# A fused attention and two feed-forward layers: sums of v spread over steps, two last tiles kept whole, next batch's attention emitted earlier

## The chip, the cores and the metric

The kernel runs on one core of a Trainium2 chip. The metric is device time in microseconds, the median of several runs. One execution was also taken by the hardware profiler; its span and rows are what is read below. The kernel is written in a tile framework: the author emits instructions in program order, and a scheduler orders them on each engine by that order and by a simulated timeline, so that an instruction emitted later may run earlier where the simulation sees a gap.

## The reference

Inputs are q, k and v of 4 batches x 12 heads x 448 positions x 64, two gain vectors, and the weights of two layers.

```python
def rmsnorm(x, g):
    return x / np.sqrt(np.mean(x * x, axis=-1, keepdims=True) + 1e-06) * g
scores = matmul(rmsnorm(q, g_q), rmsnorm(k, g_k).transpose(0, 1, 3, 2)) / np.sqrt(64)
attn = exp(scores - max(scores)); attn = attn / (sum(attn) + 1e-09)
x = matmul(attn, v)                         # to 1792 tokens x 768
h = x @ moe_w_in                            # 768 x 2048
x = (h * sigmoid(1.702 * h)) @ moe_w_out    # 2048 x 768
h = x @ moe2_w_in
out = (max(h, 0) + alpha * min(h, 0)) @ moe2_w_out
```

The kernel computes each product from 16-bit halves: an operand is scaled and split into a high and a low part (`split`, one instruction on ScalarE and one on VectorE), and three matmuls stand for one. The scales need the largest absolute value of what is scaled, for v among others, batch by batch.

## The kernel before, in words

**Attention** goes by units. A pair P of heads has four units, and each unit is a tile of 128 queries (or 64) of both heads: scores on TensorE, maximum on VectorE, exponentials on ScalarE, and for batches 1 to 3 a split and a transpose by DMA (`pt`), then `values`. The generator `attention` does one unit per step, with later phases some steps behind. The first batch is done in two halves: `first_pairs` runs units 0 and 1 of its six pairs while the first layer's input weights are converted (`w1i_steps`); a second loop over `attention` runs units 2 and 3 while the output weights (`w1o_steps`) are converted and the first 256 columns of the first layer are formed (`first_in`). Both loops have 16 steps.

**Sums of v.** For batches 1 to 3 the scale of v comes from sums of absolute values. `v_scale(b)` takes a batch in 8 pieces: a load by the POOL queue into a two-buffer tile `vst` (L312), held behind the fifth group's norms, and an Abs with a running sum on ScalarE (L313). `later_v_scales` then reduces the columns, sends them through DRAM to all partitions (`v_line`, `vrow`) and forms `mv` and `av`. All this is emitted at step 8 of the second loop.

**First layer.** `first_moe1` forms the remaining columns of the first batch's 16 tiles m and splits each, then `moe1_out` does the output product (`yp`, L812), six tiles of 48 matmuls. Activations wait in place, two tiles further on in g; for the last two tiles there is no such place, and `raw_t` gives a `last_t` of 256 columns in the buffers of `vst`, copied (L768) into a whole tile before the rest is formed.

**Order around it.** The loop at the end takes one tick of the first layer (32 for the inner tiles, 24 for the output) and emits attention steps of the next batch so far that they are done at `PACE[b]` of the 56 ticks; for the first batch they start at tick `B1_AT` = 24. `moe1` of the next batch needs all its attention (x tiles, a pool of 9 slots, `NX`).

Of the kernel before, what the change touches and what calls it, by code (L numbers as in the profile page):

```python
# [24 lines left out]
VLAG = 0  # L25
LAG_ = 4
LAG2 = 5
PACE = (1.0, 1.0, 1.0, 1.0)
HOLD = 12800
M_AT = 2  # L30
VS_AT = 8
# [26 lines left out]
def attention_moe_kernel(  # L58
# [51 lines left out]
    def scaled_reciprocal(dst, src, c):  # L110

        nc.vector.tensor_scalar(out=dst, in0=src, scalar1=1.0 / c, scalar2=None, op0=ALU.mult)
        nc.vector.reciprocal(out=dst, in_=dst)
# [24 lines left out]
    def split(dst, src, scale):  # L138

        nc.scalar.activation(out=dst[0], in_=src, func=AF.Copy, scale=scale)  # L140
        nc.vector.scalar_tensor_tensor(  # L141
            out=dst[1], in0=src, scalar=scale, in1=dst[0], op0=ALU.mult, op1=ALU.subtract
        )
# [162 lines left out]
    def v_scale(b):  # L306
        flat = v[b].rearrange("h s d -> (h s d)").rearrange("(p n) -> p n", p=128)
        n = flat.shape[1] // VN
        col = vcols[:, b - 1]
        for i in range(VN):  # L310
            t = raw_p.tile([128, n], F32, tag="vst", name="vst")
            nc.gpsimd.dma_start(out=t, in_=flat[:, i * n:(i + 1) * n])  # L312
            nc.scalar.activation(out=t, in_=t, func=AF.Abs, accum_out=col[:, i:i + 1])  # L313

    def later_v_scales():
        n = B - 1
        one = small.tile([128, B - 1], F32, tag="vone", name="vmax")
        nc.vector.tensor_reduce(out=one, in_=vcols, op=ALU.max, axis=AX)
        pow2floor(one, one)
        line = dram.tile([128, n], F32, name="v_line")  # L320
        row = att_p.tile([128, 128 * n], F32, tag="sq", name="vrow", bufs=SQB)
        nc.sync.dma_start(out=line, in_=one)
        nc.sync.dma_start(out=row, in_=line.rearrange("p b -> (p b)").partition_broadcast(128))
        nc.vector.tensor_reduce(out=mv[:, 1:B], in_=row.rearrange("q (p b) -> q b p", b=n), op=ALU.max, axis=AX)
        scaled_reciprocal(av[:, 1:B], mv[:, 1:B], 2.0 ** 13)

    raws = {}
    rawv = {}
# [197 lines left out]
        probs[u] = (sp, nm, n)  # L526

    sums_of = {}
    spread = {}

    def exponent(u):
        sp, nm, n = probs[u]
        P, half, _, _ = unit(u)
        pr = [att_p.tile([128, S], F32, tag="p", name="pr", bufs=4) for _ in range(n)]
        if u < 4 * NP:
            if u % 2 == 0:
                sums_of[P, half] = small.tile([128, 4], F32, tag="sums", name="sums", bufs=3)
            sm = sums_of[P, half][:, 2 * (u % 2):2 * (u % 2) + n]
        else:
            sm = small.tile([128, 2], F32, tag="sm", name="sm", bufs=4)[:, 0:n]  # L540
        for i in range(n):
            nc.scalar.activation(  # L542
                out=pr[i], in_=sp[:, i, 0:S], func=AF.Exp, bias=nm[:, i:i + 1],
                scale=c_s if u >= 4 * NP else 1.0, accum_out=sm[:, i:i + 1]
            )
        if u >= 4 * NP:
            nc.scalar.activation(out=sm, in_=sm, func=AF.Copy, scale=2.0 ** -14, bias=1e-9 * 2.0 ** -14)
        elif u % 2:
            sm = sums_of[P, half][:, 0:2 + n]
            nc.vector.tensor_scalar(out=sm, in0=sm, scalar1=1e-9, scalar2=None, op0=ALU.add)  # L550
            nc.vector.reciprocal(out=sm, in_=sm)
        probs[u] = (pr, sm)
# [180 lines left out]
    def urgent(on):  # L733
        return tc.high_priority(on) if on else ExitStack()

    def first_in(cols, m, g, t):

        n = cols.stop - cols.start
        ps = ps_m.tile([128, n], F32, tag="m", name="hp")
        i = 0  # L740
        for kk in range(KD):
            for e, f in ((0, 0), (0, 1), (1, 0)):
                nc.tensor.matmul(  # L743
                    out=ps, lhsT=w1i[:, kk, e, m * 128:(m + 1) * 128], rhs=xs[0, kk][:, f, cols], start=(i == 0),
                    stop=(i == 3 * KD - 1)
                )
                i += 1
        dst = raw_t(g, m)[:, cols] if t is None else t[:, cols]
        if t is None:
            t = work.tile([128, S], F32, tag="t", name="t")  # L750
        with urgent(HP0):
            nc.scalar.activation(out=t[:, cols], in_=ps, func=AF.Tanh, scale=c_t[:, 0:1])
            nc.vector.scalar_tensor_tensor(out=dst, in0=t[:, cols], scalar=1.0, in1=ps, op0=ALU.add, op1=ALU.mult)  # L753
# [7 lines left out]
    def first_moe1(g):  # L761

        for m in range(KF):
            if m < KF - 2:
                first_in(slice(FIRST, S), m, g, None)
            else:
                t = work.tile([128, S], F32, tag="t", name="t")
                nc.vector.tensor_copy(out=t[:, 0:FIRST], in_=raw_t(g, m))  # L768
                first_in(slice(FIRST, S), m, g, t)
            if m == RAW0 - 1:  # L770
                for _ in w1o_steps:
                    pass
                split_g(g, range(RAW0))
            elif m >= RAW0:
                split_g(g, (m,), t if m >= KF - 2 else None)
            yield
            yield
        yield from moe1_out(0, g)
# [47 lines left out]
    def raw_t(g, m):  # L826

        if m < KF - 2:
            return g[:, m + 2].rearrange("p e t -> p (e t)").bitcast(F32)
        if m not in last_t:  # L830
            last_t[m] = raw_p.tile([128, FIRST], F32, tag="vst", name="last_t")
        return last_t[m]

    def split_g(g, ms, t=None):
        for m in ms:
            split((g[:, m, 0], g[:, m, 1]), raw_t(g, m) if t is None else t, scales["w1o"][1][:, m:m + 1])

    TICKS = 2 * KF + 4 * KD

# [330 lines left out]
    if True:  # L1170
# [36 lines left out]
            load_qk(P)  # L1207
        load_v(2)
        normalize(1)
        for _ in first_pairs():  # L1210
            for _ in range(W_RATE):
                next(w1i_steps, None)
        for _ in w1i_steps:
# [9 lines left out]
        for i, _ in enumerate(steps):  # L1223
            pairs = max(0, (i - LAG + 1) // 2)
            rows = KF - 2 if pairs >= 4 else (HOLD + pairs * HELD) // (2 * DM) - 2
            while n1o < min(1 + 2 * rows + 3 * (rows // 2), (i + 1) * W1O_RATE, 57):
                next(w1o_steps)
                n1o += 1
            if i >= M_AT and i - M_AT < KF:
                first_in(slice(0, FIRST), i - M_AT, g0, None)  # L1230
            if i == VS_AT:
                for b in range(1, B):
                    with tc.issue_after(rooted[4].ins):
                        v_scale(b)
                later_v_scales()
        while n1o < 57:
            next(w1o_steps)
            n1o += 1
        for m in range(len(range(2 * NP + LAG)) - M_AT, KF):
            first_in(slice(0, FIRST), m, g0, None)  # L1240
        with tc.issue_after(loads["w1o"][W1O_HOLD].ins):
            normalize(NP, NP + 1)
            for _ in prep_pair(NP):
# [52 lines left out]
```

## Time and profile before

| | us |
|---|---|
| median of 3 runs | 1156.42 |
| lowest, highest | 1152.11, 1162.04 |
| profiled execution, its own time | 1151.71 |
| span of the profile, first to last instruction | 1149.9 |

Busy in the span: TensorE 1058.2 us (92%), VectorE 804.3 (70%), ScalarE 680.6 (59%), GpSimd 176.7 (15%). A share of the whole span is an average over stages, so the rows below are taken by stretches. Rows of waits give the time that an engine stood idle and what ended that time.

### The profile page before, as it was taken

To read this page: it belongs to the slowest core of one execution; us is meant where nothing else is said; L and a number is where in the kernel's file an instruction comes from. 1 tells how busy PE (TensorE), PEld (TensorE's weight loads), DVE (VectorE), ACT (ScalarE), POOL (GpSimd) and SP (SyncE) were. 2 spreads that over 40 slices of the span, in tenths; PEclk is the share of its full clock that TensorE was granted. 3 is DMA by queue.
4 is the path that set the end of the run, shared out by engine and by line. 5 is a ranking of instruction groups with operands and counts; after the bars stand their busy time and mean duration, and the time that the engine had idled before them with its cause. 6 is when DMAs were issued, how large, how long until landed. Compare 5 with 4: busy or idle time off the path is not lost.

```text
span 1149.9 us, 18349 instructions
## 1 busy us (share of the span) xinstructions
PE 1058.2 (92%) x6752; PEld 579.9 (50%) x6752; DVE 804.3 (70%) x1392; ACT 680.6 (59%) x1396; POOL 176.7 (15%) x364
## 2 busy tenths in 40 slices
PE   3576898887979999999999999999999999999998
PEld 1343466643434554555555455444444477666664
DVE  6979899987868984577533956599977223968341
ACT  4688786877888876688632562356555324655220
POOL 2622003766424332200000000000000000000000
PEclk9677999999989999999999999999999999999999
DMA  7975553378886656644436701665442323363011
GB/s 228 273 196 144 168 150 105 97 145 186 187 173 137 149 126 153 126 109 110 88 112 210 243 1 64 222 216 188 158 156 83 137 70 113 101 186 104 32 32 28
DMA packets 235562, 158.25 MB, mean 138 GB/s; under 512 B 167888, under 2 KB 214736, under 8 KB 235472
## 3 DMA queue, kind: packets, MB, share of 16 engines
q1 hardware_dynamic: 229200, 141.41, 44.3%
q0 software_dynamic: 6272, 15.67, 5.6%
q8 instruction: 53, 0.87, 0.3%
q14 instruction: 37, 0.30, 0.1%
HBM read 92.41 MB, written 25.69 MB: 103 GB/s over the span
## 4 chain that ended last, share of the span: by engine, by line
PE 55%; DVE 16%; DMA 9%; issue 9%; POOL 5%; ACT 5%; SPq 1%; ACTq 0%; POOLq 0%; DVEq 0%
PE op L1078 17%; PE yp L812 13%; PE h L918 11%; PE hp L789 8%; PE xp L639 2%; PE sp L518 2%; DMA t<-hl 2%; DVE ph L611 2%; DMA vst<-in_v_dram 1%; DMA pt<-ph 1%; DVE ss L416 1%; DVE nm L523 1%; DVE g L141 1%; PE hp L743 1%; ACT pr L542 1%
## 5 line engine op out<-in xcount | busy, mean ns | idle before, releaser
L812 PE MATMUL yp<-g,w1o 128*128 128x448 f16 x1152 | 225.4, 353 | 0.4 <-DVE g L141 0.4
L918 PE MATMUL h<-x,w2i 128*128 128x512 f16 (+1 forms) x1152 | 218.9, 352 | 2.5 <-DVE pos L924 1.4
L789 PE MATMUL hp<-x,w1i 128*128 128x448 f16 x864 | 170.8, 354 | 1.0 <-DVE t L798 1.0
L918 PEld LDWEIGHTS <-w2i 128*128 128x128 f16 x1152 | 112.7, 98 | 107.6 <-issue 3.0
L812 PEld LDWEIGHTS <-w1o 128*128 128x128 f16 x1152 | 109.8, 98 | 108.5 <-issue 8.7
L789 PEld LDWEIGHTS <-w1i 128*128 128x128 f16 x864 | 82.1, 98 | 83.8 <-issue 10.4
L523 DVE TENSOR_REDUCE nm<-sp 128x2 f32<-128x896 f32 x96 | 92.7, 966 | 13.3 <-PE sp L518 12.6
L611 DVE SCALAR_TENSOR_TENSOR ph<-pr,sm,ph 128x448 f16<-128x448 f32 x126 | 85.5, 712 | 18.6 <-ACT ph L584 18.4
L542 ACT ACTIVATE pr<-sp,nm,c_s 128x448 f32<-128x448 f32 x126 | 89.9, 716 | 4.6 <-DVE ph L611 3.3
L923 ACT ACTIVATE pos<-h,sign 128x512 f32<-128x512 f32 (+1 forms) x64 | 40.1, 628 | 87.7 <-PE h L918 81.9
L1078 PEld LDWEIGHTS <-even 128*128 128x128 f16 x672 | 65.7, 98 | 43.4
L924 DVE SCALAR_TENSOR_TENSOR pos<-h,slope,pos 128x512 f32<-128x512 f32 (+1 forms) x64 | 43.6, 683 | 60.4 <-ACT pos L923 60.4
L584 ACT ACTIVATE ph<-pr,sm 128x448 f16<-128x448 f32 x126 | 77.4, 658 | 13.8 <-DVE sm L581 13.4
L743 PE MATMUL hp<-x,w1i 128*128 128x256 f16 (+1 forms) x576 | 61.1, 263 | 9.7 <-DVE g L753 7.0
L1078 PEld LDWEIGHTS <-odd 128*128 128x128 f16 x504 | 49.3, 98 | 32.6
L1078 PE MATMUL op<-w2lo,even 128*128 128x384 f16 x384 | 63.4, 326 | 0.0
L639 PE MATMUL xp<-pt,vs 128*64 128x256 f16 (+1 forms) x792 | 49.7, 268 | 14.8 <-DMA pt<-ph 13.5
L743 PEld LDWEIGHTS <-w1i 128*128 128x128 f16 x576 | 52.1, 99 | 20.3 <-issue 17.2
L518 PE MATMUL sp<-t 64*128 64x448 f16 (+1 forms) x432 | 54.7, 360 | 3.0 <-ACT pr L542 3.0
L639 PEld LDWEIGHTS <-vs 128*64 128x64 f16 x792 | 37.6, 112 | 33.5 <-issue 15.3
L525 ACT ACTIVATE nm<-nm,c_s 128x2 f32<-128x2 f32 x72 | 20.8, 289 | 50.7 <-DVE nm L523 50.5
L1078 PE MATMUL op<-w2hi,even 128*128 128x384 f16 x288 | 47.5, 326 | 0.0
(242 smaller groups left out, 1644.9 us busy)
## 6 DMA issues: line engine op xcount, KB each, us to landing
g<-in_moe_w_in_dram SPq DMA_DIRECT2D x24, 512.0 KB, 5.5
g<-in_moe_w_out_dram SPq DMA_DIRECT2D x32, 384.0 KB, 3.9
w2raw<-in_moe_w_in_dram SPq DMA_DIRECT2D x24, 512.0 KB, 5.3
w2raw<-in_moe_w_out_dram SPq DMA_DIRECT2D x16, 768.0 KB, 6.4
g_dram<-pos SPq DMA_DIRECT2D x48, 256.0 KB, 2.0
gp<-g_dram SPq DMA_DIRECT2D x8, 1024.0 KB, 6.5
odd<-g_dram SPq DMA_DIRECT2D x6, 1024.0 KB, 5.4
y_dram<-y SPq DMA_DIRECT2D x24, 224.0 KB, 2.2
```

Of the source, the lines that this page charges most:

```text
L518: nc.tensor.matmul(out=sp[:, j, 0:S] if n == 2 else sp[ds, 0, 0:S], lhsT=qt[ds] if n == 2 else qt[ds, 64:128], rhs=kt[ds, 0:S], start=(i = ...
L523: nc.vector.tensor_reduce(out=nm[:, 0:n], in_=sp[:, 0:n, 0:S], op=ALU.max, axis=AX, negate=True)
L542: nc.scalar.activation(out=pr[i], in_=sp[:, i, 0:S], func=AF.Exp, bias=nm[:, i:i + 1], scale=c_s if u >= 4 * NP else 1.0, accum_out=sm[:, ...
L584: nc.scalar.activation(out=ph[:, i, 0:S], in_=pr[i], func=AF.Copy, scale=sm[:, i:i + 1])
L611: nc.vector.scalar_tensor_tensor(out=ph[:, i, S:2 * S], in0=pr[i], scalar=sm[:, i:i + 1], in1=ph[:, i, 0:S], op0=ALU.mult, op1=ALU.subtract)
L639: nc.tensor.matmul(out=xp[64 * j:64 * j + 64, t:t + n], lhsT=vs[ks, j, c], rhs=pt[ks, 7 * j + kc, 0:n] if b else pt[ks, kc, o:o + n], star ...
L743: nc.tensor.matmul(out=ps, lhsT=w1i[:, kk, e, m * 128:(m + 1) * 128], rhs=xs[0, kk][:, f, cols], start=(i == 0), stop=(i == 3 * KD - 1))
L789: nc.tensor.matmul(out=ps, lhsT=w1i[:, kk, e, m * 128:(m + 1) * 128], rhs=x[:, f], start=(n == 0), stop=(n == 3 * KD - 1))
L812: nc.tensor.matmul(out=ps, lhsT=w1o[:, m, e, j * 128:(j + 1) * 128], rhs=g[:, m, f], start=(n == 0), stop=(n == 3 * KF - 1))
L918: nc.tensor.matmul(out=ps, lhsT=w2i[:, kk, e, m * 128:(m + 1) * 128], rhs=x2[kk][:, f], start=(c == 0), stop=(c == 3 * KD - 1))
L924: nc.vector.scalar_tensor_tensor(out=pos, in0=ps, scalar=slope[:, m:m + 1], in1=pos, op0=ALU.mult, op1=ALU.max)
L1078: nc.tensor.matmul(out=ps, lhsT=ops[:, o, m, f], rhs=rhs[:, e], start=(c == 0), stop=(c == 3 * KH - 1))
```

## The change

There are three edits. The sums of v become a generator `measures` that does one piece at a time: one per step of the first loop from step 6 on, two per step of the second, and the final reduction after the last. Each load keeps its place behind the norms, and each Abs is now also ordered behind the exponentials most recently emitted (`steady[-1]`). The last two tiles of activations get whole tiles of 448 columns from the pool of x, so that the copy and the tile that it filled go, as does the parameter that passed it. And `PACE[0]` is 0.85 in place of 1.0.

```diff
-PACE = (1.0, 1.0, 1.0, 1.0)
+PACE = (0.85, 1.0, 1.0, 1.0)
...
             t = raw_p.tile([128, n], F32, tag="vst", name="vst")
-            nc.gpsimd.dma_start(out=t, in_=flat[:, i * n:(i + 1) * n])
-            nc.scalar.activation(out=t, in_=t, func=AF.Abs, accum_out=col[:, i:i + 1])
+            with tc.issue_after(rooted[4].ins):
+                nc.gpsimd.dma_start(out=t, in_=flat[:, i * n:(i + 1) * n])
+            with tc.issue_after(steady[-1].ins):
+                nc.scalar.activation(out=t, in_=t, func=AF.Abs, accum_out=col[:, i:i + 1])
+            yield
...
+    def measures():
+        for b in range(1, B):
+            yield from v_scale(b)
+        later_v_scales()
...
-            nc.scalar.activation(
+            last = nc.scalar.activation(
                 out=pr[i], in_=sp[:, i, 0:S], func=AF.Exp, bias=nm[:, i:i + 1],
                 scale=c_s if u >= 4 * NP else 1.0, accum_out=sm[:, i:i + 1]
             )
+        steady.append(last)
...
-        dst = raw_t(g, m)[:, cols] if t is None else t[:, cols]
-        if t is None:
-            t = work.tile([128, S], F32, tag="t", name="t")
+        dst = raw_t(g, m)[:, cols]
+        t = work.tile([128, S], F32, tag="t", name="t")
...
-            if m < KF - 2:
-                first_in(slice(FIRST, S), m, g, None)
-            else:
-                t = work.tile([128, S], F32, tag="t", name="t")
-                nc.vector.tensor_copy(out=t[:, 0:FIRST], in_=raw_t(g, m))
-                first_in(slice(FIRST, S), m, g, t)
+            first_in(slice(FIRST, S), m, g)
...
-            last_t[m] = raw_p.tile([128, FIRST], F32, tag="vst", name="last_t")
+            last_t[m] = big.tile([128, S], F32, tag="x", name="last_t", bufs=NX)
...
-        for _ in first_pairs():
+        measure = measures()
+        for i, _ in enumerate(first_pairs()):
+            if i >= 6:
+                for _ in range(1):
+                    next(measure, None)
             for _ in range(W_RATE):
                 next(w1i_steps, None)
...
-                first_in(slice(0, FIRST), i - M_AT, g0, None)
-            if i == VS_AT:
-                for b in range(1, B):
-                    with tc.issue_after(rooted[4].ins):
-                        v_scale(b)
-                later_v_scales()
+                first_in(slice(0, FIRST), i - M_AT, g0)
+            if i >= 0:
+                for _ in range(2):
+                    next(measure, None)
+        for _ in measure:
+            pass
```

## Rows read from the trace of the kernel before

**Rows 1.** Busy time of each engine by stretches, with TensorE's clock and DMA's share.
```profile
core 0: us, PE busy (x) PEld busy (x) DVE busy (x) ACT busy (x) POOL busy (x), PEclk, DMA share, GB/s
45.00:119.00 74.00, 50.07 (x284) 26.38 (x283) 61.44 (x124) 57.28 (x142) 19.86 (x45) 0.77 0.69 192
119.00:200.00 81.00, 69.90 (x602) 49.87 (x601) 74.94 (x182) 60.05 (x139) 9.93 (x20) 1.00 0.48 134
200.00:236.00 36.00, 29.65 (x277) 23.02 (x277) 34.48 (x65) 28.34 (x64) 26.22 (x36) 0.95 0.34 84
236.00:341.00 105.00, 87.24 (x665) 43.18 (x664) 79.16 (x127) 83.94 (x210) 49.28 (x88) 0.96 0.87 178
341.00:560.00 219.00, 218.65 (x1523) 109.68 (x1522) 161.19 (x270) 171.22 (x399) 51.01 (x107) 1.00 0.59 129
```
**Rows 2.** ScalarE's waits, 45 to 119 us: total us, times, longest.
```profile
ACT vst L313 <- DMA vst<-in_v_dram: 14.3, 7, 3.7
```
**Rows 3.** VectorE's waits in the same stretch.
```profile
DVE w1o L164 <- ACT w1o L148: 5.2, 3, 3.9
DVE g L164 <- ACT g L148: 3.4, 2, 2.9
```
**Rows 4.** Timeline of ScalarE: start, length, instruction, idle time before it.
```profile
80.58 0.48 ACT L313 ACTIVATE vst<-vst 128x336 f32<-128x336 f32 x1 [3.58 <-DMA vst<-in_v_dram]
80.97 0.19 ACT L313 ACTIVATION_READ_ACCUMULATOR vst<-vst 128x1 f32 x1
```
**Rows 5.** Timeline of VectorE, the same columns.
```profile
67.19 1.09 DVE L451 TENSOR_TENSOR qn<-qk,rs 128x896 f32<-128x896 f32 x1 [0.20 <-issue]
...
81.74 0.43 DVE L164 TENSOR_SCALAR g<-g 128x512 int32<-128x512 int32 x1 [2.88 <-ACT g L148]
```
**Rows 6.** TensorE's waits, 236 to 341 us.
```profile
PE xp L639 <- DMA pt<-ph: 13.5, 7, 4.5
```
**Rows 7.** Timeline of TensorE, 236 to 341 us; xp starts a pair's values.
```profile
241.91 1.18 PE L639 MATMUL xp<-pt,vs 128*64 128x256 f16 x18 [3.73 <-DMA pt<-ph]
...
327.42 2.07 PE L812 MATMUL yp<-g,w1o 128*128 128x448 f16 x10
...
329.79 0.74 PE L639 MATMUL xp<-pt,vs 128*64 128x256 f16 x10
...
336.52 0.37 PE L639 MATMUL xp<-pt,vs 128*64 128x192 f16 x1 [4.54 <-DMA pt<-ph]
```
**Rows 8.** The Abs of the pieces of v: count, ns, first and last start.
```profile
L313 ACT ACTIVATE vst<-vst x24: 465/492/599, 53.3 to 123.5; 128x336 f32<-128x336 f32 x24
```
**Rows 9.** The loads of the pieces: issue, and time to landing.
```profile
L312 POOL DMA_DIRECT2D vst<-in_v_dram x24: 536/536/770, 48.8 to 115.9; - x24
...
DMA to landing us min/median/max: 2.5/3.3/8.9
```
**Rows 10.** Timeline of VectorE: the final reduction, the first use of its scale.
```profile
152.97 0.68 DVE L324 TENSOR_REDUCE mv<-vrow 128x3 f32<-128x384 f32 x1 [1.09 <-DMA vrow<-v_line]
...
178.72 0.75 DVE L141 SCALAR_TENSOR_TENSOR vs<-vr,av,vs 128x512 f16<-128x512 f32 x1
```
**Rows 11.** Timeline of POOL.
```profile
60.67 0.22 POOL L427 TENSOR_TENSOR rs<-tn,rs 128x14 f32<-128x14 f32 x1
...
179.92 0.73 POOL L387 DMA_DIRECT2D vr<-in_v_dram  x1 [63.46 <-DMA vs<-vs]
...
226.88 3.64 POOL L437 TENSOR_TENSOR qk<-qk,rs 128x896 f32<-128x896 f32 x2
230.67 2.35 POOL L471 TENSOR_TENSOR hl<-qk,hl 128x896 f16<-128x896 f32 x1
```
**Rows 12.** Timeline of VectorE at the two copies.
```profile
224.81 0.67 DVE L611 SCALAR_TENSOR_TENSOR ph<-pr,sm,ph 128x448 f16<-128x448 f32 x1
...
227.21 3.47 DVE L768 COPY t<-last_t 128x256 f32<-128x256 f32 x2
...
231.19 2.30 DVE L611 SCALAR_TENSOR_TENSOR ph<-pr,sm,ph 128x448 f16<-128x448 f32 x1
```
**Rows 13.** Busy time of the output layer's matmuls (L812) in the stretch.
```profile
core 0: us, PE busy (x) PEld busy (x), PEclk, DMA share, GB/s
...
236.00:341.00 105.00, 52.12 (x259) 23.68 (x257) 0.96 0.87 178
```

More of the change, by code (lines that the diff above doesn't have):

```diff
@@ L528, in attention_moe_kernel @@
     sums_of = {}
+    steady = []
     spread = {}
@@ L734, in urgent, with first_in @@
         return tc.high_priority(on) if on else ExitStack()
-    def first_in(cols, m, g, t):
+    def first_in(cols, m, g):
         n = cols.stop - cols.start
@@ L774, in first_moe1 @@
             elif m >= RAW0:
-                split_g(g, (m,), t if m >= KF - 2 else None)
+                split_g(g, (m,))
             yield
@@ L830, in raw_t, with split_g @@
         if m not in last_t:
-            last_t[m] = raw_p.tile([128, FIRST], F32, tag="vst", name="last_t")
+            last_t[m] = big.tile([128, S], F32, tag="x", name="last_t", bufs=NX)
         return last_t[m]
-    def split_g(g, ms, t=None):
+    def split_g(g, ms):
         for m in ms:
-            split((g[:, m, 0], g[:, m, 1]), raw_t(g, m) if t is None else t, scales["w1o"][1][:, m:m + 1])
+            split((g[:, m, 0], g[:, m, 1]), raw_t(g, m), scales["w1o"][1][:, m:m + 1])
     TICKS = 2 * KF + 4 * KD
@@ L1239, in attention_moe_kernel @@
         for m in range(len(range(2 * NP + LAG)) - M_AT, KF):
-            first_in(slice(0, FIRST), m, g0, None)
+            first_in(slice(0, FIRST), m, g0)
         with tc.issue_after(loads["w1o"][W1O_HOLD].ins):
```

## The prediction

> **What bounds the kernel now.** I read the busy time by stretches first, because the share of the whole span (TensorE 92%) hides that the stages have different limits. From 341 us on TensorE is never idle [rows 1]: what happens to the other engines there is worth nothing, and all that can be won lies before. In 45 to 119 us TensorE is busy for 50 of 74 us, VectorE for 61.44 and ScalarE for 57.28 [rows 1], so no engine looks full. The waits say otherwise: ScalarE stood for 14.3 us at the head of its queue because a piece of v had not landed [rows 2], and 57.28 + 14.3 = 71.6 of 74 us: ScalarE, with its stalls, is the bound of this stretch. That is seen from the other side in VectorE's waits, which go to ScalarE's conversions of weights: 5.2 and 3.4 us [rows 3]. One such pair shows it best: ScalarE waits 3.58 us for v at 80.58 us [rows 4], and VectorE waits for the ScalarE conversion behind it (2.88 us at 81.74) [rows 5]. The clock granted there is 0.77 on average, but TensorE doesn't set this stretch.
>
> From 119 to 236 us VectorE is the bound: 74.94 of 81 us and 34.48 of 36 us [rows 1]. From 236 to 341 us the second batch's attention runs with the first batch's output layer as filling. No engine is full: TensorE 87.24, ScalarE 83.94, VectorE 79.16 of 105 us, but the DMA engines stand at 0.87 [rows 1], and TensorE's 13.5 us of waits there go to transposes that have not landed [rows 6]. At 329.79 us the output layer's matmuls have run out (the last ten begin at 327.42), and a late transpose then leaves TensorE idle for 4.54 us with nothing to put there [rows 7].
>
> **The change part by part.**
>
> *Sums of v.* The 24 pieces, their loads and their 24 Abs instructions all stay: one takes 0.58 us from its start at 80.58 us to the end of its accumulator's read [rows 4], 14 us in all. What changes is where. Now the scheduler fits them in wherever it believes a load has come, from 53.3 to 123.5 us [rows 8], with two buffers to load into. After the change each is pinned behind the exponentials of its step. One per step from step 6 of the first half: the next load of that buffer is issued as soon as the Abs is done and has two steps to land, against 2.5/3.3/8.9 us (least, median, most) [rows 9]. The ten steps from the sixth on fill most of the 74 us, by my estimate 6 us each. So the stall of 14.3 us should go nearly wholly there. What is late next is VectorE: its 61.44 us of work, at the idle share of the next two stretches (6.06 of 81 and 1.52 of 36, 7.5% and 4.2%, mean 5.9%) [rows 1], need 65.3 us in place of 74. I take -8.7 us; the ends are -9.9 (4.2% idle) and -3 (most stalls come back elsewhere).
>
> In the second half 14 pieces come at two per step. Its 16 steps fill the 81 us of the stretch, 5 us each; a pair needs two POOL issues and a landing, about 1.1 + 3.3 = 4.4 us from [rows 9], so the median fits and the longest doesn't. About eight Abs (4.6 us) move out of 45 to 119 into a stretch where ScalarE has 21 us free and VectorE is the bound: +0.5 (0 to 4). The final reduction then comes later against its surroundings. It stalls VectorE for 1.09 us now, and VectorE first uses it at 178.72, 26 us after [rows 10]; I take +0.5 (-1 to +3).
>
> The queues that it passes: on POOL, the chain of pair 5's norms ends at 60.67 us behind four loads of v, and is needed at 67.19 [rows 5, 11], so a load that waits two or three us longer for its Abs still costs nothing, and six or more would show. Afterwards POOL has nothing until 179.92, where it had been waiting 63.46 us [rows 11]; the later loads fit in there. On SP only the two small transfers of the maxima move, among the weight loads.
>
> *Last activations whole.* Two copies, 3.47 us together on VectorE, leave a stretch that VectorE bounds [rows 12]. Nothing is added: the two tiles take slots of the pool of x, of which six hold the first batch, and the one that is left is enough until the first layer frees the six. But the copies' price isn't all theirs. POOL runs two multiplications in just those us, 3.64 for both [rows 11], and the next VectorE instruction with two inputs, beside POOL's following subtraction of 2.35 us, takes 2.30 us where the same form takes 0.67 a little earlier [rows 11, 12]. The engines wait for each other, and without the copies another instruction may pay. If one instruction pays that difference, 1.63 us, 1.84 of the 3.47 are won, if two do, 0.2: I take -1.8, between -0.2 and -3.5. The Trainium skill (SBUF — State Buffer, Who interferes with whom) has a rule that speaks against the edit: VectorE's two-port copies, and also its instructions with two SBUF inputs while GpSimd reads SBUF, share one port pair with GpSimd under a lock held for a whole instruction. Both rows agree with it. By that rule alone the splits that move up would inherit nearly the whole wait, this term would stand near -0.2, and the sum below would come to 1146.3.
>
> *Pace 0.85.* The second batch's 29 attention steps start at tick 24 as before, but are spread over 23.6 ticks in place of 32. Ten instead of eight are then emitted ahead of the last first-layer tile. A tick of the output layer is 12 matmuls of 52.12/259 = 0.201 us [rows 13]. Between two steps there were 32/29 x 12 = 13.2 of them, 2.66 us, and there will be 9.8, 1.96 us: 2.8 us less in a pair of four steps. The pair now takes (329.79 - 241.91)/5 = 17.6 us [rows 7]; with TensorE's idle time kept it would take 14.8. ScalarE's work in a pair is 83.94/105 x 17.6 = 14.1 us, the DMA engines' 0.87 x 17.6 = 15.3 [rows 1], so DMA comes last and adds 0.5 us of idle TensorE to each of six pairs, +3. In return 8.4 ticks, 20 us of output-layer matmuls, are left when the attention ends, so that the 4.5 us of idle tail [rows 7] are filled. The work itself is only displaced, since TensorE is full afterwards. Two steps earlier also means transposes in 200 to 236, where DMA stands at 0.34 [rows 1], which I put at -0.7 (a quarter of the 2.8 us by which the filling shrinks). Net -2.2; the ends are -4.5 (nothing but the tail changes) and +12.3 (the pair stays at 17.6 us, 6 x 2.8 idle less 4.5).
>
> *Sum:* -8.7 + 0.5 + 0.5 - 1.8 - 2.2 = -11.7 us. The profiled execution took 1151.71 us (a span of 1149.9), so it would come to 1140.0; the median of the runs, 1156.42, to **1144.7**. Before's own runs lie 10 us apart, so I treat 1% (11.6 us) as what a measurement can tell from no change.
>
> **The rivals.**
> - *Full gain.* VectorE packs as in 200 to 236 (-9.9), the copies' wait vanishes with them (-3.5), the tail goes (-4.5), and the earlier transposes also take the 3.73 us that TensorE waits at 241.91 [rows 7]: -21.6, **1134.8**. For it: free DMA in 200 to 236. Against: VectorE is full there, and it makes what the transposes carry.
> - *The stalls come back in the second half.* With two buffers and two pieces a step, a landing over about 4 us stalls ScalarE, and VectorE behind it. If half of seven pairs lose 4 us and two thirds of that reach VectorE, 9 of the 11.7 us are given back: **1153.7**. For it: landings up to 8.9 us [rows 9]. Against: DMA is at 0.48 there, 0.69 in 45 to 119 [rows 1].
> - *Slower: attention emitted too early.* If the transposes hold the pair at 17.6 us whatever TensorE is given, the thinner filling leaves TensorE idle: +12.3. The two extra steps also put VectorE work (79.16/24 = 3.3 us each) ahead of the last splits, on which the output layer's first accumulation rests: up to +6.6 of TensorE with nothing to do. With -8.7 + 1 - 1.8 that is +9.4, **1165.8**. It decides as soon as the pair stays above some 17.1 us, where the idle time (6 x 2.3 - 4.5) eats the 9.5 us that the rest brings. For it: DMA at 0.87 and 13.5 us of waits for transposes. Against: these waits are seven, not one per pair and step, and DMA isn't yet full.
>
> **How the numbers follow.** Forecast 0.48, full gain 0.24, stalls back 0.13, slower 0.15. The forecast stands on the 1% line, so its chance is split 0.27 over and 0.21 within. Full gain adds 0.24 to faster, stalls back 0.13 to the same; of the slower case 0.05 is within 1% and 0.10 beyond. Faster 0.51, same 0.39, slower 0.10. The range goes from just below the full gain, 1130, to 1162, within which most of the slower case's span (without the 6.6 it gives 1159.2) still lies.
>
> **What would show it.** In the profile after: ScalarE's waits for v under 3 us up to the first split of x; VectorE over 90% busy in the stretch from 45 us to that split, which begins near 110 us in place of 118; no copy at the last two tiles, and POOL's multiplications beside splits of 1.4 us or more in their place; the pair's period at 15 to 16 us, output-layer matmuls still there when the last values of the second batch are formed, and TensorE unbroken from about 330 us. The prediction is wrong if ScalarE's waits for v only move behind 119 us, if another wait (weights from DMA, POOL's norms) fills the 8.7 us, or if TensorE's waits for transposes grow over the 13.5 us.

## The result and the profile after

The changed kernel takes 1169.58 us (median of 6) against 1152.82 us (median of 6): a ratio of 1.0134, 95% interval 1.0103 to 1.0164. It is slower by over 1%, and 7.6 us above the range's upper end. (The 1156.42 from which the prediction starts is the median of the first three of the six runs of the kernel before.) Its profiled execution took 1169.68 us, a span of 1167.8.

The second layer's input product (matmuls `h<-x,w2i`) begins at 750.5 us in place of 732.8, 17.7 us later, and the spans differ by 17.9: all of it is lost before. The stretches that answer to [rows 1] are cut here where the changed kernel's stages end. Busy time by stretches, first the kernel before:

```profile
core 0: us, PE busy (x) PEld busy (x) DVE busy (x) ACT busy (x) POOL busy (x), PEclk, DMA share, GB/s
45.00:117.00 72.00, 48.07 (x270) 25.24 (x270) 60.61 (x122) 56.19 (x138) 19.86 (x45) 0.76 0.68 189
117.00:206.00 89.00, 76.36 (x669) 55.32 (x668) 81.62 (x203) 64.79 (x147) 12.64 (x24) 1.00 0.49 136
206.00:245.00 39.00, 30.46 (x274) 21.29 (x272) 34.90 (x57) 30.64 (x72) 24.50 (x33) 0.96 0.51 106
245.00:335.00 90.00, 77.75 (x589) 38.34 (x587) 71.46 (x113) 75.33 (x189) 48.29 (x87) 0.98 0.85 178
335.00:420.00 85.00, 83.23 (x582) 41.23 (x583) 72.19 (x123) 71.85 (x170) 30.98 (x65) 0.96 0.68 148
```

The same view of the changed kernel:

```profile
45.00:117.00 72.00, 53.64 (x306) 27.72 (x305) 62.18 (x127) 56.66 (x131) 17.95 (x39) 0.86 0.65 171
117.00:206.00 89.00, 70.66 (x556) 49.03 (x555) 74.72 (x179) 61.53 (x149) 13.92 (x29) 0.94 0.51 144
206.00:245.00 39.00, 30.26 (x289) 25.53 (x289) 32.95 (x60) 27.35 (x67) 24.69 (x36) 0.85 0.44 90
245.00:335.00 90.00, 76.10 (x551) 37.16 (x548) 68.59 (x106) 67.21 (x166) 47.21 (x80) 0.96 0.78 165
335.00:420.00 85.00, 80.62 (x581) 40.04 (x580) 69.20 (x120) 71.47 (x172) 27.50 (x56) 0.96 0.67 146
```

Read TensorE's counts (the numbers behind x) roughly as work done. The first stretch does 36 matmuls more, the second 113 fewer, the third 15 more, the fourth 38 fewer. From 45 to 420 us, 2283 matmuls are begun in place of 2384, 101 fewer; at the last stretch's 0.143 us (83.23/582) to an output-layer matmul's 0.201 [rows 13], that is 14 to 20 us, the whole loss. It has two places: the second half of the first batch's attention, and the second batch's attention.

ScalarE's waits from 45 to 117 us, with the totals that answer to [rows 2], then those for v from 117 to 206:

```profile
ACT w1o L148 <- DMA g<-in_moe_w_in_dram: 7.8, 4, 3.2
ACT g L148 <- DMA g<-in_moe_w_in_dram: 3.1, 2, 2.5
ACT vst L315 <- DMA vst<-in_v_dram: 2.4, 2, 1.7
...
ACT vst L315 <- DMA vst<-in_v_dram: 1.6, 1, 1.6
```

The waits for v did go, as predicted. In their place ScalarE waits 10.9 us for the input weights (7.8 + 3.1), where the kernel before waits 1.1. Two of these waits can be followed to SP, which issues the weights' loads. SP takes its transfers in order and stands 6.6 us at `row<-line`, the reload of a small store that has not landed yet:

```profile
SPq L129 <- DMA line<-am: 6.6, 1, 6.6
...
74.18 0.33 SPq L129 DMA_DIRECT2D row<-line  x1
74.61 10.50 SPq L223 DMA_DIRECT2D g<-in_moe_w_in_dram  x3
...
81.91 0.67 ACT L148 ACTIVATE g<-g 128x512 f32<-128x512 f32 x1 [2.53 <-DMA g<-in_moe_w_in_dram]
83.59 0.68 ACT L148 ACTIVATE g<-g 128x512 f32<-128x512 f32 x1 [0.54 <-DMA g<-in_moe_w_in_dram]
```

The loads behind this reload are issued from 74.61 us on, and ScalarE waits for the first two of them at 81.91 and 83.59. The kernel before stands at the same reload for 7.4 us. So what is late next, once v is out of the way, is not an engine's work but SP's queue, at least in part.

The Abs answer to [rows 8], and the split of x was to begin near 110 us:

```profile
L315 ACT ACTIVATE vst<-vst x24: 466/488/542, 63.5 to 146.8; 128x336 f32<-128x336 f32 x24
...
L140 ACT ACTIVATE x<-xraw,first_sc x6: 492/496/498, 116.3 to 121.9; 128x256 f16<-128x256 f32 x6
```

The split begins at 116.3 in place of 118.4: 2.1 us won where 8.7 were forecast. The last Abs starts 23 us later than before.

How one short stall spreads in the second half: timelines of POOL, ScalarE, TensorE and VectorE of the changed kernel, picked from 128 to 146 us.

```profile
130.88 0.54 POOL L313 DMA_DIRECT2D vst<-in_v_dram  x1 [1.76 <-ACT vst L315]
...
133.76 0.48 ACT L315 ACTIVATE vst<-vst 128x336 f32<-128x336 f32 x1 [1.63 <-DMA vst<-in_v_dram]
...
136.32 0.44 PE L575 MATMUL rp<-identf,sums 128*64 128x128 f32 x4 [3.53 <-ACT ptf L614]
...
138.41 3.11 PE L753 MATMUL hp<-x,w1i 128*128 128x256 f16 x18
...
141.55 0.47 ACT L761 ACTIVATE t<-hp,c_t 128x256 f32<-128x256 f32 x1 [2.81 <-PE hp L753]
...
142.58 0.42 DVE L667 SCALAR_TENSOR_TENSOR own<-xp,first_sc,own 128x192 f32<-128x192 f32 x1 [2.64 <-PE xp L649]
...
143.73 2.12 PE L753 MATMUL hp<-x,w1i 128*128 128x256 f16 x18 [0.25 <-ACT ptf L614]
```

POOL can issue a load only when an earlier Abs has left the buffer, so ScalarE stands 1.63 us for it; TensorE then waits 3.53 us for a copy that is queued on ScalarE behind this; its next 18 matmuls take 3.11 us where the same 18 take 2.12 a little later; ScalarE waits for them (2.81), and VectorE (2.64) for the values that TensorE forms behind them. The granted clock from 117 to 206 us is 0.94 in place of 1.00.

The second place, 214 to 231 us, on POOL, ScalarE, VectorE and TensorE:

```profile
214.75 0.61 POOL L382 DMA_DIRECT2D qk<-in_q_dram  x1
...
220.89 0.58 ACT L422 ACTIVATE sq<-qk 128x448 f32<-128x448 f32 x1 [3.01 <-DMA qk<-in_q_dram]
...
221.50 0.62 DVE L424 TENSOR_REDUCE ss<-sq 128x7 f32<-128x448 f32 x1 [3.19 <-ACT sq L422]
...
222.81 2.53 DVE L141 SCALAR_TENSOR_TENSOR g<-g,ratio_w1o 128x448 f16<-128x448 f32 x1
...
226.86 0.34 DVE L762 SCALAR_TENSOR_TENSOR g<-t,hp 128x192 f32<-128x192 f32 x1
...
227.25 3.04 PE L753 MATMUL hp<-x,w1i 128*128 128x192 f16 x18 [5.37 <-DVE g L762]
```

ScalarE and behind it VectorE stand at a later pair's norms. POOL has issued the last load of that pair's k and q at 214.75 us, and ScalarE's wait for it ends at 220.89. The activation that TensorE needs is queued behind these norms and behind a split of 2.53 us: 5.37 us of idle TensorE, where the longest such wait in the same stretch of the kernel before was 2.2.

What TensorE's clock does at both places (its two levels are 1.2 and 2.4 GHz, so 0.50 is the lower one throughout):

```profile
136.30:141.50 5.20, 5.18 (x36) 3.38 (x37) 2.90 (x9) 2.44 (x9) 1.07 (x2) 0.67 0.39 108
141.50:146.00 4.50, 4.11 (x36) 2.92 (x35) 3.42 (x6) 3.39 (x7) 0.00 (x0) 1.00 1.01 321
...
227.20:231.50 4.30, 4.25 (x25) 2.83 (x25) 3.62 (x5) 4.19 (x12) 3.49 (x9) 0.50 0.58 114
```

Behind both idle times the granted clock is low, so that they cost more than their own length.

The first layer's tiles end at 244.2 us in place of 229.1, and the pair then has a period of 19.3 us ((345.63 - 248.93)/5), against 17.6 [rows 7].

### The profile page after: what moved, and what is told of

It reads as the page before. It is cut to its first block, busy times and chain, and to the rows that moved or that the text cites. A ratio compares the mean times of both kernels' runs of the same rounds, so it can differ in the third digit from the quotient of the medians.

```text
span 1167.8 us, 18353 instructions
## 1 busy us (share of the span) xinstructions
PE 1070.9 (92%) x6752; PEld 586.1 (50%) x6752; DVE 806.2 (69%) x1390; ACT 680.5 (58%) x1396; POOL 179.4 (15%) x364
## 4 chain that ended last, share of the span: by engine, by line
PE 60%; DVE 14%; DMA 11%; issue 6%; ACT 4%; POOL 2%; SPq 0%; ACTq 0%; POOLq 0%; DVEq 0%
PE op L1082 16%; PE yp L816 14%; PE hp L793 11%; PE h L922 10%; PE xp L649 3%; PE sp L526 3%; DMA pt<-ph 2%; DMA g<-in_moe_w_out_dram 1%; DVE nm L531 1%; DMA qk<-in_q_dram 1%; DMA g<-in_moe_w_in_dram 1%; DVE g L141 1%; DMA vst<-in_v_dram 1%; DVE w2num L165 1%; DVE ph L621 1%
## 5 line engine op out<-in xcount | busy, mean ns | idle before, releaser
L816 PE MATMUL yp<-g,w1o 128*128 128x448 f16 x1152 | 228.1, 355 | 0.5 <-DVE g L141 0.4
L793 PEld LDWEIGHTS <-w1i 128*128 128x128 f16 x864 | 82.3, 98 | 83.0 <-issue 8.9
L621 DVE SCALAR_TENSOR_TENSOR ph<-pr,sm,ph 128x448 f16<-128x448 f32 x126 | 88.6, 736 | 23.6 <-ACT ph L594 23.6
L753 PE MATMUL hp<-x,w1i 128*128 128x256 f16 (+1 forms) x576 | 67.0, 279 | 16.8 <-DVE g L762 10.8
L753 PEld LDWEIGHTS <-w1i 128*128 128x128 f16 x576 | 56.4, 105 | 28.0 <-issue 22.9
L649 PE MATMUL xp<-pt,vs 128*64 128x256 f16 (+1 forms) x792 | 50.7, 268 | 18.2 <-DMA pt<-ph 17.2
L649 PEld LDWEIGHTS <-vs 128*64 128x64 f16 x792 | 38.3, 112 | 37.9 <-issue 17.5
```

The source lines that it names most:

```text
L621: nc.vector.scalar_tensor_tensor(out=ph[:, i, S:2 * S], in0=pr[i], scalar=sm[:, i:i + 1], in1=ph[:, i, 0:S], op0=ALU.mult, op1=ALU.subtract)
L649: nc.tensor.matmul(out=xp[64 * j:64 * j + 64, t:t + n], lhsT=vs[ks, j, c], rhs=pt[ks, 7 * j + kc, 0:n] if b else pt[ks, kc, o:o + n], star ...
L753: nc.tensor.matmul(out=ps, lhsT=w1i[:, kk, e, m * 128:(m + 1) * 128], rhs=xs[0, kk][:, f, cols], start=(i == 0), stop=(i == 3 * KD - 1))
L793: nc.tensor.matmul(out=ps, lhsT=w1i[:, kk, e, m * 128:(m + 1) * 128], rhs=x[:, f], start=(n == 0), stop=(n == 3 * KD - 1))
L816: nc.tensor.matmul(out=ps, lhsT=w1o[:, m, e, j * 128:(j + 1) * 128], rhs=g[:, m, f], start=(n == 0), stop=(n == 3 * KF - 1))
```

## The experiments

**One edit at a time.** The first three split the change.

*Pace undone, in the changed kernel, and pace alone, in the kernel before:*
```diff
-PACE = (0.85, 1.0, 1.0, 1.0)
+PACE = (1.0, 1.0, 1.0, 1.0)
```


> The changed kernel with PACE[0] back at 1.0; sums of v and whole tiles stay. Theory 'early attention' (the second batch's attention stands ahead of the last first-layer tiles on VectorE and costs most of the loss of 17 us): about 1153 to 1158, with the output layer's first matmul back near 230 us. Theory 'sums' (the Abs in the second half delay that half's weights, and all after it): still above 1163. Theory 'order' (any edit reshuffles the planned order and costs or wins some us by itself): anything between 1150 and 1172, not equal to what the single edits add up to.

> The kernel before with PACE[0] = 0.85 and nothing else. 'Early attention': 1163 to 1170, slower than before by 10 us or more, with the stretch to 200 us as before. 'Sums': within 3 us of before (1153). 'Order': a moderate shift of either sign.

Undone: 1.0177 (1.0152 to 1.0202). Alone: 0.9996 (0.9977 to 1.0015). Pace is not the loss, and alone it shows no gain (the interval reaches 2.7 us down). In both pairs of traces every engine, TensorE and SP too, runs the same instructions in the same order with and without it, as far as line, tile name and shape tell. So nothing shows that the step from 1.0134 to 1.0177, whose intervals overlap, is its doing.

*Whole last tiles alone, in the kernel before:*
```diff
...
-                t = work.tile([128, S], F32, tag="t", name="t")
-                nc.vector.tensor_copy(out=t[:, 0:FIRST], in_=raw_t(g, m))
-                first_in(slice(FIRST, S), m, g, t)
+            first_in(slice(FIRST, S), m, g, None)
...
+            last_t[m] = big.tile([128, S], F32, tag="x", name="last_t", bufs=NX)
```


> The kernel before with the last two tiles kept whole and nothing else. 'Early attention' and 'sums' alike: -0.2 to -3.5 us against before, as forecast for the two copies. 'Order': a shift beyond that, of either sign, with the stretch to 200 us changed too though none of the edit lies in it.

1.0001 (0.9976 to 1.0025). No gain is seen; the interval reaches 2.8 us down, so that it excludes the end of -3.5, but not -1.8. POOL's multiplications and VectorE beside them, in this run:

```profile
231.14 3.98 POOL L437 TENSOR_TENSOR qk<-qk,rs 128x896 f32<-128x896 f32 x2
235.08 2.26 POOL L471 TENSOR_TENSOR hl<-qk,hl 128x896 f16<-128x896 f32 x1
...
232.07 1.51 DVE L141 SCALAR_TENSOR_TENSOR g<-g,ratio_w1o 128x448 f16<-128x448 f32 x1 [0.52 <-ACT g L140]
233.50 4.33 DVE L611 SCALAR_TENSOR_TENSOR ph<-pr,sm,ph 128x448 f16<-128x448 f32 x2
```

The two splits take 4.33 us for work of 2 x 0.67 [rows 12]: they pay what the copies paid.

*Sums of v alone* (the pieces as in the change, with both other edits undone):

> The kernel before with the sums of v spread and nothing else. 'Early attention': 1144 to 1153, no slower than before. 'Sums': 1158 to 1165, with ScalarE's waits for v small but the last weight split (203.9 us before) 5 us or more later. 'Order': either sign, with waits for other things than v.

1.0145 (1.0121 to 1.0170), the whole loss. The rest varies this kernel.

**What the first half could give.** *All pieces left out, from the kernel before* (24 loads and Abs; a constant stands for the sums, the reduction stays):
```diff
-                for b in range(1, B):
-                    with tc.issue_after(rooted[4].ins):
-                        v_scale(b)
+                nc.vector.memset(vcols, 32.0)
```


> The kernel before with the 24 loads and Abs left out and their sums set to a constant; the reduction stays at step 8. It shows what the pieces cost in all. By the forecast's reading (ScalarE and its 14.3 us of waits bound the stretch to 119 us): 1140 to 1146. If the loads of the input weights come last instead, as the changed kernel's waits of 10.9 us say: 1150 to 1156, with the first split of x at 113 us or later.

0.9990 (0.9964 to 1.0016). Even with no Abs at all, the first split of x only comes forward from 118.4 to 115.6 us:

```profile
L140 ACT ACTIVATE x<-xraw,first_sc x6: 493/496/502, 115.6 to 120.5; 128x256 f16<-128x256 f32 x6
...
ACT g L148 <- DMA g<-in_moe_w_in_dram: 6.6, 2, 5.3
...
ACT w1o L148 <- DMA g<-in_moe_w_in_dram: 3.4, 3, 2.8
```

ScalarE waits for input weights instead, and 6.0 us for VectorE (3.1 and 2.9):

```profile
ACT w1o L148 <- DVE w1i L180: 3.1, 1, 3.1
ACT w1i L179 <- DVE inv_w1i L172: 2.9, 2, 1.5
...
SPq L129 <- DMA line<-am: 7.1, 1, 7.1
```

SP stands at the same reload as above. As far as the scheduler leaves the rest alone, this run is the measure of what any placement of the sums can win: 1.2 us, with an interval from 4.2 us won to 1.8 lost.

**Spread, or ordered?** *Sums alone without the order behind exponentials:*
```diff
-            with tc.issue_after(steady[-1].ins):
-                nc.scalar.activation(out=t, in_=t, func=AF.Abs, accum_out=col[:, i:i + 1])
+            nc.scalar.activation(out=t, in_=t, func=AF.Abs, accum_out=col[:, i:i + 1])
```


> The sums alone, at the changed kernel's steps, but each Abs free of the order behind the exponentials. 'Pin': 1150 to 1158, with ScalarE's waits for v back at 10 us or more. 'Second half': also back near 1155 if the scheduler again pulls the pieces ahead of 125 us, and 1165 or more if it leaves them where they are emitted; the first start and the last start of the Abs tell which.

0.9983 (0.9957 to 1.0008): the scheduler puts the Abs back where they were (53.5 to 123.7 us against 53.3 to 123.5). All that the spreading does, it does through that order. The same with all three edits:

> The changed kernel (all three edits) with the Abs not ordered behind exponentials; their loads keep their place behind the norms, and the emission is still spread. All theories that put the loss on the pin: 0.995 to 1.002. If the three edits hold something of their own together (whole tiles and pace win once the sums do no harm): 0.990 to 0.996. If spreading the emission costs in itself: 1.005 or more.

1.0001 (0.9981 to 1.0022).

*All pieces in the first half* (three per step of the first loop in place of one):

> The sums alone on the kernel before, at three pieces a step of the first loop and so ended before the second loop begins. Theory 'second half' (14 pieces, or the reduction that ends them, in the half that converts the output weights cost the 16 us): back to 1150 to 1157. Theory 'pin' (the order behind the exponentials costs wherever it stands): 1165 or more. Theory 'order' (any change of these instructions' place reshuffles the rest): not told.

1.0152 (1.0104 to 1.0199), and the loss lies in another place: the first half takes longer, and the split of x begins at 141.2 us in place of 118.4.

**The queue of the maxima.** In the changed kernel SP stood 10.6 us with the store of the maxima at its head, among the weight loads, then 1.8 us with the reload. *Reload four steps after the store, in the kernel with the sums alone:*
```diff
         nc.sync.dma_start(out=line, in_=one)
+        for _ in range(8):
+            yield
         nc.sync.dma_start(out=row, in_=line.rearrange("p b -> (p b)").partition_broadcast(128))
```


> The sums alone, with four steps between the store of the maxima and their reload, so that SP's queue doesn't stand still for the store to land. Theory 'SP' (a store, its landing of 4 us and a reload stand one behind the other in the queue of the weight loads, which the chain shows at 150 to 160 us): 1158 to 1164, 5 to 10 us back. 'Second half' by the pieces themselves: no change from 1172 within 3 us.

1.0049 (1.0024 to 1.0075): SP still stood 11.4 us at the store, yet 11 of 17 us were regained (1.0145 to 1.0049). *Both transfers on POOL* (`nc.gpsimd` for `nc.sync`), with the sums alone and with all three edits:

> The sums of v alone (pinned, spread over both halves, as in the changed kernel), with the store of the maxima and its reload issued by POOL in place of SP. Theory 'head of SP's queue' (SP stands about 10.5 us at the store and 2 to 3 us at the reload without issuing loads of output weights, and the second half falls behind by that): SP issues the weights without a gap, the last column group of the first layer ends within 5 us of 229 us in place of 243, and the ratio to before is 0.997 to 1.005. Theory 'other order' (pinning the Abs makes the scheduler lay out both halves differently, whatever queue carries the maxima): ratio 1.012 to 1.018 as with SP, the last first-layer matmuls still near 243. Theory 'pinned Abs' (the Abs themselves, waiting behind exponentials, hold ScalarE's conversions): also 1.01 or more, with ScalarE's waits, not SP's, ahead of VectorE's idle time in the second half.

> The changed kernel (all three edits) with the store of the maxima and its reload on POOL. Theory 'head of SP's queue': 0.995 to 1.004 of before, since whole tiles alone and pace alone came to 1.000 each. Theory 'other order' or 'pinned Abs': 1.010 to 1.016, as the changed kernel.

1.0179 (1.0150 to 1.0209) and 1.0201 (1.0161 to 1.0241). The theory of SP's queue falls. TensorE, VectorE and ScalarE run the same instruction sequences as with SP; the loss stays with these sequences, whoever carries the maxima.

**Which part of the ordered sums.** Each edit is made in the kernel with the sums alone. *Only the fourteen of the second half ordered; the fourteen left out, loads and Abs (a constant stands for their sums); the reduction left out (a constant stands for its result); three loads for 24, one for the eight Abs of a batch:*
```diff
+            with tc.issue_after(steady[-1].ins) if b * VN + i >= VN + 10 else ExitStack():
...
+            if b * VN + i >= VN + 10:
+                yield
+                continue
...
+        nc.vector.memset(mv[:, 1:B], 32.0)
...
-        later_v_scales()
...
+            if i == 0:
+                t = raw_p.tile([128, n], F32, tag="vst", name="vst")
```


> The sums of v alone, with only the fourteen Abs of the second half ordered behind exponentials; the first ten are free. Theory 'second half' (what costs is Abs and loads that stand in ScalarE's and POOL's queues after 117 us): ratio 1.010 to 1.016, as with all 24 ordered. Theory 'first half' (the order that the ten ordered Abs force on the first half costs): 0.998 to 1.004. Theory 'late reduction' (the maxima, ready 22 us later, cost wherever the Abs stand): 1.010 to 1.016 too, told apart by the next two.

> The sums of v alone with the fourteen pieces of the second half left out, loads and Abs; the first ten are ordered behind exponentials as in the changed kernel, and the reduction stays, with nothing late to wait for. Theories 'second half' and 'late reduction': 0.997 to 1.004, first layer's first part over near 229 us. Theory 'first half': 1.010 to 1.016.

> The sums of v alone, all 24 Abs ordered behind exponentials, but the final reduction left out (maximum, the two transfers, the second maximum; a constant stands for the result). Theory 'late reduction': 0.997 to 1.004. Theory 'second half': 1.010 to 1.016 still, with the stalls of ScalarE and the waits of TensorE for it where they were (about 131 to 141 us).

> The sums of v alone with three loads in place of 24: the eight Abs of a batch go over the same loaded piece, in the same order behind the exponentials, and the reduction stays. Theory 'second half' as a matter of loads (ScalarE at the head of its queue for a piece that has not landed, 2 us at 131 us, and POOL behind it): 0.997 to 1.005. If the Abs themselves cost by their place in ScalarE's order, or the late reduction: 1.010 to 1.016.

Fourteen ordered: 1.0036 (1.0014 to 1.0057). Fourteen left out: 0.9991 (0.9964 to 1.0017). No reduction: 1.0050 (1.0033 to 1.0068). Three loads: 0.9981 (0.9964 to 0.9999). With three loads, the last of them at 96.7 us, nothing is lost, though all 24 Abs stand in the same order behind exponentials. But two edits that keep the second half's loads give back about two thirds (no reduction) and three quarters (fourteen ordered) of the 1.45%, which no theory expected: the parts don't add up to a sum.

**Lateness, or the sequences?** *Changed kernel with each Abs behind one unit earlier* (`steady[-2]`); *sums alone with only the first ten ordered; changed kernel with the pieces begun at step 5 in place of 6:*

> The changed kernel (all three edits) with each Abs ordered behind the exponentials of one unit earlier, the last but one emitted. The work is the same and the sums can end a unit earlier (about 2 to 5 us before 147). Theory 'lateness' (the loss grows with how late the last pieces and the maxima are): 1.008 to 1.014, a little less than the changed kernel. Theory 'laid-out order' (the instruction orders that the scheduler fixes around these constraints stall each other, and a small shift gives other orders): anything from 1.000 to 1.016, out of proportion to the few us by which the sums end earlier.

> The sums of v alone with only the first ten Abs ordered behind exponentials, the fourteen of the second half free; they stay behind the ten because the two buffers are handed on in order. Theory 'second half's loads' (the ten keep the buffers, so the fourteen loads fall behind 117 us whether their Abs are ordered or not): 1.010 to 1.016, as with all 24 ordered. If it is the ordering of the fourteen itself: 0.998 to 1.004.

> The changed kernel with the pieces started at step 5 in place of 6, so that eleven fall in the first half and thirteen in the second. Theory 'lateness': 1.009 to 1.015. Theory 'laid-out order': anything from 1.000 to 1.016.

1.0035 (1.0008 to 1.0061), 1.0037 (1.0019 to 1.0054), 1.0032 (1.0016 to 1.0049). The work is the same, and in the last two the Abs end as late as in the changed kernel. All three lie below what lateness alone was to give, and the second below what the loads alone were to give (1.010 to 1.016). That the order is what counts was a theory that allowed anything from 1.000 to 1.016: these runs refute its rivals rather than prove it. The third, by stretches:

```profile
117.00:206.00 89.00, 70.57 (x552) 48.91 (x552) 73.56 (x174) 60.61 (x145) 13.92 (x28) 0.92 0.47 133
206.00:245.00 39.00, 33.50 (x340) 26.39 (x339) 35.12 (x71) 32.38 (x78) 25.82 (x36) 0.97 0.49 113
245.00:335.00 90.00, 82.93 (x604) 39.69 (x602) 73.92 (x117) 75.84 (x185) 50.95 (x87) 0.96 0.82 184
```

It loses as much in the second half as the changed kernel (552 matmuls against 556), and makes it up afterwards. All in one table; the last column is POOL's wait of the second batch's norms (`ss`) for VectorE's `inv_w1o`, between 185 and 215 us, a mark of which sequence ran and not a cost (in most kernels marked `none`, POOL waits 3.9 to 6.0 us for the same `inv_w1o` with a load of q and k):

| kernel | ratio | last Abs, us | matmuls 117-206, 206-245, 245-335 | POOL's wait, us |
|---|---|---|---|---|
| before | 1 | 123.5 | 669, 274, 589 | none |
| changed | 1.0134 | 146.8 | 556, 289, 551 | 5.7 |
| pace undone | 1.0177 | 149.5 | 538, 283, 561 | 5.7 |
| sums alone | 1.0145 | 146.0 | 537, 303, 540 | 5.7 |
| same, maxima on POOL | 1.0179 | 147.6 | 531, 286, 561 | 5.7 |
| all edits, maxima on POOL | 1.0201 | 146.0 | 543, 315, 528 | 5.7 |
| reload apart | 1.0049 | 148.8 | 574, 276, 629 | none |
| fourteen ordered | 1.0036 | 146.8 | 574, 327, 617 | none |
| no reduction | 1.0050 | 147.2 | 557, 335, 603 | none |
| one unit earlier | 1.0035 | 138.2 | 584, 298, 621 | none |
| ten ordered | 1.0037 | 147.4 | 576, 298, 616 | none |
| from step five | 1.0032 | 146.2 | 552, 340, 604 | 2.2 |
| fourteen left out | 0.9991 | 103.9 | 605, 299, 601 | none |
| three loads | 0.9981 | 140.4 | 583, 337, 575 | none |

The five kernels that lose more than 1% share the mark of 5.7 us and do at most 561 matmuls in the last stretch; the others reach 575 and more. So the loss is two things. Sums that end late in the second half, with their loads: +0.3 to 0.5% (six kernels; that it is the loads rests on the two edits without them, which changed the sequences too). And one set of instruction sequences, which the scheduler settled on in these five: about 1% more. The five have the same edit of the sums, and TensorE's order is the same in all of them from start to end, so they are one layout, but for the copies and the queue of the maxima, measured five times. Small shifts of the pieces, or a reload elsewhere, gave other sequences.

The cleanest pair is sums alone (1.0145) against ten ordered (1.0037). Every load of v is issued within 1.3 us of the same time, and every Abs begins within 2.5 us of it; ScalarE's order is the same up to 142 us, VectorE's up to 146 and TensorE's up to 212. What differs between the two is the order behind that, and with it 1.1%. TensorE's clock doesn't set the five apart: from 117 to 420 us it is 0.94 in the changed kernel, but also 0.94 with the fourteen left out and 0.93 without the reduction (0.98 before).

## Why the prediction was wrong

**What bounds the kernel, and the -8.7.** Failed. The step was "57.28 + 14.3 = 71.6 of 74 us: ScalarE, with its stalls, is the bound of this stretch". The stall was real and went (2.4 us left), but the input weights came only a little later: their loads stand in SP's queue behind a reload (6.6 us), which the prediction did not look at. I named VectorE as next after the stall; the loads were, and the prediction's own list of what would make it wrong had them. Leaving all pieces out measures the term: 0.9990, or -1.2 us (-4.2 to +1.8) where -8.7 was forecast. VectorE stood at 62.18 of 72 us, 86%, not over 90.

**The fourteen pieces and the reduction, +0.5 each.** Failed in size, and most of the loss lies here. "The median fits and the longest doesn't" held as a statement on one stall: there was one, of 1.63 us. But I priced each wait by its own length, and took 4 and 3 us as upper ends. Each engine takes its instructions in order and hands a wait on (1.63, 3.53, 2.81, 2.64 us), and the late sums cost 4 to 6 us in the six kernels with other sequences (0.32 to 0.50% of 1153). The other 1% wasn't in the sum at all: the scheduler's reaction to a new ordering constraint, which the prediction put at nothing by taking all other instructions to stay where they were. "On SP only the two small transfers of the maxima move" passed over a wait of 10.6 us at the head of SP; the runs on POOL show that it wasn't the cause.

**Last activations whole, -1.8.** No copies remained, and no gain is seen (1.0001); the interval can't tell -0.2 from -1.8, but the rows speak for -0.2. VectorE's splits beside POOL's work took 4.33 us for 1.34, and one took 2.53 us in the changed kernel (222.81). The Trainium skill (SBUF — State Buffer, Who interferes with whom) describes an exclusive lock on a port pair that the two engines share, and the prediction worked out from it that the splits inherit the copies' wait. The trace agrees: the 4.33 us stand where the copies stood, beside the same two multiplications of POOL. One reading of the rows was loose: the split at 231.19 us in the kernel before was not the next one after the copies; another ran at 230.60 in 0.67 us, just ahead of POOL's subtraction.

**Pace 0.85, -2.2.** Measured alone at 0.9996, which doesn't exclude -2.2 by itself. But neither the price nor the gain shows in the trace: the pair's period stayed at 17.5 us ((331.93 - 244.41)/5), and the last ten of the output layer's matmuls begin at 329.56, where they began at 327.42 [rows 7]. I had taken the emission's spacing for the spacing on the engine; the scheduler put the output layer's matmuls between the steps in the same order as before. The transposes' waits of TensorE grew in the changed kernel (17.2 us from 247 to 372, against 13.5 in the shorter stretch of [rows 6]), but with pace undone too (17.8 us).

**The rivals.** "The stalls come back in the second half" had the right place, and its 1153.7 was 9 us above the forecast; in the six kernels with late sums but other sequences the time is 1157 to 1160, so its direction was right, its price still too small, since nothing had been won before it. "Attention emitted too early" gave 1165.8, near the measured 1169.6, by a mechanism that isn't there: pace alone costs nothing. That the scheduler would lay out other sequences was not among the rivals.

**Open.** Which of the shared sequences' waits cost the 1% was not separated; the wait at 220 to 227 us is one, and the slower pairs follow. No run fixed a sequence by hand. No version beat the kernel before by more than 0.2%: the lowest ratio, 0.9981 (0.9964 to 0.9999), leaves out 21 loads. No run took the reload at which SP stands out of the way of the input weights.

## What to carry to other kernels

Price a stall by leaving the stalled work out altogether; one such run estimates what any rearrangement of it can win, and here that was 1.2 us, not clear of zero. Where a scheduler fixes each engine's order from an estimated timeline, an ordering constraint on a side task is not local: the same work one unit earlier cost 0.35% in place of 1.34%, so measure two or three neighbouring placements before you give a placement the credit or the blame. Count matmuls by stretch in both traces: that shows where time is lost for good and where a later stage makes it up.

## What the runs showed of the hardware

A short idle time of TensorE costs more than itself: behind 3.53 us of waiting, 18 matmuls took 3.11 us where the same form took 2.12, at a granted clock of 0.67 in place of 1.00 (136.3 to 141.5 us against 141.5 to 146). Nine more loads of 168 KB between 117 and 206 us went with only slightly slower weight loads there, 25 of them: their median landing was 3.7 us before and 4.1 after. VectorE's splits with two inputs in SBUF took 1.5 to 2.5 us each beside POOL's work in the rows shown, and 0.67 us without it.
